# Gathered rows of x transposed by SyncE DMA instead of TensorE, with smaller key, value and query buffers, in a retention + top-1 expert kernel

## The chip, the cores and the metric

The kernel runs on one core of one Trainium2 chip. The metric is the device time of one execution in microseconds (us), lower is better. Three executions of the kernel before took 371.51, 374.61 and 376.12 us; the median is 374.61. Each profile shows one execution.

The engines are named as the profile names them: PE is TensorE (matmuls; PEld its weight loads), DVE is VectorE, ACT is ScalarE, POOL is GpSimd and SP is SyncE, which only issues DMAs here.

## What is computed

```python
# attention without softmax, 8 batches x 8 heads x 576 tokens x 64
scores = scale * np.matmul(q, k.transpose(0, 1, 3, 2))
Dmat = np.where(rel >= 0, gamma[:, None, None] ** rel[None, :, :], 0.0)   # decay by distance
attn_out = np.matmul(scores * Dmat[None], v)
x = attn_out.transpose(0, 2, 1, 3).reshape(4608, 512)

# one expert of eight for each token
logits = x @ w_gate
expert_idx = np.argmax(logits, axis=1)          # gate_w: that expert's softmax probability
for e in range(8):
    mask = expert_idx == e
    h = np.maximum(x[mask] @ w1[e], 0.0)        # 512 -> 1024
    out[mask] = gate_w[mask, None] * (h @ w2[e])  # 1024 -> 512
```

All inputs and the output are float32 in HBM. The kernel keeps x as bf16 rows in HBM (`x_rows`), and the experts work in bf16.

## The kernel before, in words

The kernel has two stages, written out in a fixed order: each engine runs its instructions in the order in which the program issues them, and no scheduler moves them.

**Attention stage (0 to about 202 us).** Forty blocks are walked: 8 batches, each four blocks of 128 tokens and one of 64. The loop at L693 runs block i, and in it prepares later blocks. POOL multiplies queries and keys by their decay (`scale_q` L244, `scale_k` L254), PE transposes the scaled tiles (`stage_TQ`, `stage_TK`), forms scores (`stage_SC`, output `pssc`, masked by DVE into `sc` at L311), the running state (`stage_S`, output `pss`) and the result (`stage_AV` and `stage_IN`, output `psx`), and turns that into rows (`stage_R`), which ACT copies into `xr` tiles (L397, L398) and SP writes to `x_rows` (L399, L405). SP also loads everything: keys for block i+6 early in iteration i (`load_k`, ordered after the latest mask step), values for block i+6 late (`load_v`, ordered after the latest copy of the result), and half a batch of queries at two places in each batch (`load_q`, two batches ahead). The pools are `ldq` (2 tiles of a whole batch), `ldk` (7 key tiles and 7 value tiles) and smaller working pools.

The logits are computed as the blocks come (`stage_L1`, `stage_L2`). When the first half of the batches is done, the routing of the first half of the tokens runs in small steps between the blocks (`route_first`, L655): the best expert for each token, the token's rank within its expert, and tables of row numbers (`tidg`) for each expert. Then, in four steps with a block between them, POOL gathers the rows of experts 0 to 3 (`gather`, an indirect DMA at L637 for each 128 rows into a tile `xg` of 128 x 512 bf16, pool `gath` of 8 tiles). From the last seven blocks on POOL also issues loads of the experts' weights, which convert to bf16 on the way.

**Expert stage (about 202 to 366 us).** It has sixteen units (`seq`, L745): each expert has a unit of 256 rows (ph 0, tokens of the first half) and one of 384 rows (ph 1, the rest). First come (0,0) to (3,0), then (0,1) to (3,1), then both units of experts 4 to 7. One unit is:

- `trans` (L756): for each 128 rows, PE transposes four 128 x 128 pieces of `xg` into PSUM (`pt`, pool `psT`, 2 buffers) and DVE copies them to `xt` (L764);
- `mm1` (L767): 32 matmuls `pm<-xt,w1b`, with ACT's ReLU into `ht` (L780), PSUM pool `psH` with 3 buffers;
- `mm2` (L784): 8 matmuls for each 128 rows, `py<-w2b,ht`; DVE multiplies by the gate into `ys` (L794), and POOL scatters the rows to the output (L795).

The order in PE's queue is `mm1` of a unit, `trans` of the next unit, `mm2` of the unit, except that the unit (0,1) is transposed after `mm2` of (3,0). The routing of the second half of the tokens (`route_rest`) runs on DVE and PE in small steps inside the first four units; its tables are needed to gather any ph 1 unit. After it, `gather` is called for (0,1) and (1,1), and from unit 4 on each unit i gathers the rows of unit i+2, behind `mm1`. Weights of experts 4 to 7 are fetched two loads per unit from the start of the stage (`fetch`). A check at the end (L858) covers experts with more rows than fit; its branch isn't taken with these inputs.

Of the kernel before, what the change touches and what calls it, by code (L numbers as in the profile page):

```python
# [41 lines left out]
def kernel(  # L42
# [33 lines left out]

    wpool = ctx.enter_context(tc.tile_pool(name="wts", bufs=4))
    rt = ctx.enter_context(tc.tile_pool(name="route", bufs=1))
    gp = ctx.enter_context(tc.tile_pool(name="gath", bufs=8))

    p1 = ExitStack()
    ldq = p1.enter_context(tc.tile_pool(name="ldq", bufs=2))
    ldk = p1.enter_context(tc.tile_pool(name="ldk", bufs=7))
    wkp = p1.enter_context(tc.tile_pool(name="wk", bufs=2))
    wk3 = p1.enter_context(tc.tile_pool(name="wk3", bufs=3))
    wk4 = p1.enter_context(tc.tile_pool(name="wk4", bufs=4))
# [10 lines left out]

    def load_q(b, g, dep=None, eng=None):

        if g == 0:  # L100
            qts[b] = ldq.tile([P, H, NCH, DH], F32, tag="q", name="qt")
        hs = slice(g * NP, (g + 1) * NP)
        after((eng or nc.sync).dma_start(out=qts[b][:, hs, :, :],
                                         in_=q[b, hs, 0:NCH * P, :].rearrange("h (p s) d -> p h s d", p=P)), dep)

    def load_kv(store, tag, src, i, dep):
        b, c = blocks[i]
        store[i] = ldk.tile([P, H, DH], F32, tag=tag, name=tag + "t")
# [16 lines left out]
    def load_v(i, dep=None):  # L125

        if i >= NB:
            return
        b, c = blocks[i]
        if c < NCH:  # L130
            load_kv(vts, "v", v, i, dep)
            return
        vts[i] = ldk.tile([P, H, DH], F32, tag="v", name="vt")
# [107 lines left out]
    def scale_q(b, p):  # L241
        h0 = 2 * p
        qq = wkp.tile([P, NCH, P], F32, tag="qq")
        nc.gpsimd.tensor_tensor(  # L244
            out=qq[:, :, :].rearrange("p s (h d) -> p h s d", d=DH), in0=qts[b][:, h0:h0 + 2, :, :],
            in1=qg[:, 0:NCH, h0:h0 + 2].rearrange("p s h -> p h s").unsqueeze(3)
                .to_broadcast([P, 2, NCH, DH]), op=ALU.mult)
        qqs[(b, p)] = qq
# [47 lines left out]
    def stage_SC(i):  # L296
# [1 line left out]
            return  # L298
        b, c = blocks[i]
        kT = kTs.pop(i)  # L300
        sc = wkp.tile([P, 2, NP, P], F32, tag="sc")
        scs[i] = sc
        if c < NCH:
            qT = qTs[b]
# [321 lines left out]
        slots[ph] = (tids, tidg, gat)  # L626


    gat_t = {}

    def gather(e, ph):
        nb = (CA if ph == 0 else CB) // P
        nr = NTOK // 2 if ph == 0 else NTOK
        for j in range(nb):
            i = j * E + e
            xg = gp.tile([P, DM], BF16, tag="xg", name="xg")
            nc.gpsimd.indirect_dma_start(  # L637
                out=xg[:, :], out_offset=None, in_=x_rows[0:nr, :],
                in_offset=bass.IndirectOffsetOnAxis(ap=slots[ph][1][:, i:i + 1], axis=0),
                bounds_check=nr - 1, oob_is_err=False)  # L640
            gat_t[(e, ph, j)] = xg

    def steps(g, budget):

# [8 lines left out]
        return True  # L653

    def route_first():  # L655
        incl = yield from softmax_top1(0, rtmp)
        yield from ranks(0, incl, rtmp, lambda: psw.tile([P, 512], F32, tag="W", name="psrk"))
        yield from prep(0, 0, rtmp)
        yield from rows_hot(0, 0, rtmp)
        yield from place(0, rtmp, lambda: psw.tile([P, 512], F32, tag="W", name="pspl"))  # L660
        for e in range(NA):
            yield None
            gather(e, 0)
        yield from prep(1, 0, rt)
        yield from rows_hot(1, 0, rt)

# [58 lines left out]
    while steps(rf, 1.0):  # L725
# [19 lines left out]
    seq = ([(e, 0) for e in range(NA)] + [(e, 1) for e in range(NA)]  # L745
           + [(e, ph) for e in range(NA, E) for ph in (0, 1)])
    xts = {}
    wq = [(e, i) for e in range(EW, E) for i in range(4)]

    def fetch(n):  # L750
        for _ in range(n):
            if wq:
                e, j = wq.pop(0)
                load_w(e, j, 2, wpool2)

    def trans(e, ph):  # L756
        nb = (CA if ph == 0 else CB) // P
        xt = xtp.tile([P, NPT, nb * P], BF16, tag=f"xt{ph}", name="xt")
        for j in range(nb):
# [4 lines left out]
            nc.vector.tensor_copy(out=xt[:, :, j * P:(j + 1) * P], in_=pt[:, :, :])  # L764
        xts[(e, ph)] = xt

    def mm1(e, ph, between):  # L767
        nb = (CA if ph == 0 else CB) // P
# [38 lines left out]
    trans(0, 0)  # L807
    rr = route_rest()
    steps(rr, 2.0)
    routed, late = [], []  # L810

    def route_on(n):
        more = steps(rr, n)
        if not more and not routed:
            routed.append(True)
            gather(0, 1)
            if late:
                gather(*late.pop())
        return more

    for i, (e, ph) in enumerate(seq):
        nxt = seq[i + 1] if i + 1 < len(seq) else None
        fetch(2)

        def during1():
            if i < NA:
                route_on(0.9)

        def during2():
            if i < NA:  # L830
                route_on(1.2)

        ht = mm1(e, ph, during1)
        if nxt == (0, 1):
            while route_on(1):
                pass
            mm2(e, ph, ht, during2)
            trans(*nxt)
        else:
            if nxt:  # L840
                trans(*nxt)
            if i >= NA and i + 2 < len(seq):
                gather(*seq[i + 2])
            elif nxt == (NA - 1, 0):
                late.append((1, 1))
                if routed:
                    gather(*late.pop())
            mm2(e, ph, ht, during2)
    p2.close()


# [103 lines left out]
```

## Time and profile before

| | |
|---|---|
| median of three executions | 374.61 us |
| profiled execution, its own time | 381.34 us |
| its span, first to last instruction | 379.6 us |
| start of the expert stage (first `pt`) | 202.3 us |
| start of the last `py` group | 361.0 us |
| PE, DVE, ACT, POOL busy | 331.8, 156.9, 127.1, 196.9 us |
| mean granted clock of PE | 0.963 |
| DMA share 202 to 245, 245 to 290, 290 to 366 us | 0.97, 0.81, 0.28 |

Busy time is the time in which an engine has at least one instruction running; idle time of an engine that doesn't set the end costs nothing. The slices divide the span into 40 equal parts of 9.5 us, and each digit is a busy share in tenths. The DMA share is the mean busy share of the core's 16 DMA engines. In a timeline row the columns are the start in us, the length in us, the engine, the line of the program, the operation and its tiles, and, in brackets, the idle time just before and who ended it. The largest groups of DMA issues, with the median time from issue to landing where the profile has it:

```profile
kt<-in_k_dram SPq DMA_DIRECT2D x32, 256.0 KB, 4.2
qt<-in_q_dram SPq DMA_DIRECT2D x14, 512.0 KB, 5.4
x_rows<-xr SPq DMA_DIRECT2D x32, 128.0 KB, 5.5
```

### The profile page before, as it was taken

Reading aid. Unit: us, or ns where it says so; the run is one execution under the profiler, and the core shown is the slowest. Engines: PE = TensorE matmul, PEld = TensorE weight load, DVE = VectorE, ACT = ScalarE, POOL = GpSimd, SP = SyncE. Lnnn points to the kernel's source line nnn. Section 1 sums busy time; section 2 is a strip of 40 time slices with the busy share of each in tenths; the row PEclk is TensorE's granted clock in tenths of the full one; section 3 lists DMA queues with packets and bytes.
Section 4 is the critical chain, followed back from the end, with each engine's and each line's share of the span. In section 5 each row is a group of like instructions: output and inputs, shape, how many; then the busy total and the mean of one; then the engine's idle time right before and its main releaser. Section 6 shows DMA issues by size and latency. Waiting matters only on the chain.

```text
span 379.6 us, 11084 instructions
## 1 busy us (share of the span) xinstructions
PE 331.8 (87%) x4642; PEld 241.9 (64%) x4642; DVE 156.9 (41%) x358; ACT 127.1 (33%) x292; POOL 196.9 (52%) x241
## 2 busy tenths in 40 slices
PE   2499999999999999987865998799999999999950
PEld 2378788878878787875754675355556565656520
DVE  3034443434346776732587872222223232323220
ACT  2234444343354344322321321134432323232300
POOL 4884452634345452568843357547666555554230
PEclk9799999999999999999996999899999999999995
DMA  8969888889799978699999898987679222223120
GB/s 211 254 108 224 213 207 202 202 213 199 193 209 224 231 186 205 161 190 232 213 207 213 181 191 212 186 168 143 175 190 207 97 98 96 101 95 108 55 74 7
DMA packets 113083, 65.34 MB, mean 172 GB/s; under 512 B 83838, under 2 KB 105342, under 8 KB 113024
## 3 DMA queue, kind: packets, MB, share of 16 engines
q0 software_dynamic: 18176, 31.47, 38.0%
q1 hardware_dynamic: 93792, 32.02, 36.3%
q10 hardware_dynamic: 1056, 1.05, 0.9%
q8 instruction: 38, 0.62, 0.7%
q14 instruction: 21, 0.17, 0.1%
HBM read 67.14 MB, written 15.20 MB: 217 GB/s over the span
## 4 chain that ended last, share of the span: by engine, by line
PE 78%; DMA 4%; ACT 4%; DVE 4%; POOL 3%; issue 2%; another core or an unknown queue 1%; SPq 0%; ACTq 0%; POOLq 0%; DVEq 0%
PE pm L60 19%; PE py L60 18%; PE psx L60 12%; PE pssc L60 7%; PE psr L63 5%; PE psk L63 5%; PE pss L60 5%; PE psq L63 2%; PE pt L63 2%; PE psl L60 2%; DMA x_rows<-xr 1%; DMA kt<-in_k_dram 1%; DMA vt<-in_v_dram 1%; DVE xt L764 1%; ACT kT L276 1%
## 5 line engine op out<-in xcount | busy, mean ns | idle before, releaser
L780 ACT ACTIVATE ht<-pm 128x384 bf16<-128x384 f32 (+1 forms) x96 | 50.5, 526 | 105.2 <-PE pm L60 95.5
L254 POOL TENSOR_TENSOR kk<-kt,kg 128x512 f32<-128x512 f32 x40 | 41.9, 1048 | 78.0 <-PE pss L60 47.7
L60 PE MATMUL pm<-xt,w1b 128*128 128x256 bf16 (+1 forms) x512 | 74.0, 304 | 2.2 <-DVE xt L764 2.2
L795 POOL DMA_INDIRECT out_dram<-ys,tids x40 | 40.9, 1022 | 67.5 <-DVE ys L794 61.4
L60 PE MATMUL py<-w2b,ht 128*128 128x512 bf16 x320 | 73.6, 385 | 2.5 <-issue 1.6
L60 PEld LDWEIGHTS <-w1b 128*128 128x128 bf16 x512 | 50.8, 99 | 25.0 <-DVE xt L764 2.0
L60 PEld LDWEIGHTS <-ht 128*128 128x128 bf16 x320 | 31.0, 99 | 38.3 <-issue 4.3
L794 DVE TENSOR_SCALAR ys<-py,gat 128x512 f32<-128x512 f32 x40 | 30.0, 750 | 50.3 <-PE py L60 46.7
L637 POOL DMA_INDIRECT xg<-x_rows,tidg x40 | 41.5, 1037 | 14.6 <-issue 9.8
L276 ACT COPY kT<-psk 128x512 f32<-128x512 f32 x40 | 23.8, 596 | 70.5 <-PE psk L63 41.8
L311 DVE TENSOR_TENSOR sc<-pssc,mask 128x1024 f32<-128x1024 f32 x32 | 39.1, 1222 | 19.6 <-issue 13.3
L356 DVE COPY xT<-psx 128x512 f32<-128x512 f32 x32 | 22.1, 692 | 54.8 <-PE psx L60 49.7
L60 PE MATMUL psx<-sc,vt 128*64 128x128 f32 (+1 forms) x640 | 37.6, 266 | 1.0 <-DVE sc L311 1.0
L63 PE MATMUL psk<-ident,kk 128*128 128x128 f32 x160 | 27.5, 294 | 11.9 <-POOL kk L254 11.3
L60 PE MATMUL pssc<-qT,kT 64*64 64x128 f32 (+1 forms) x1024 | 36.5, 255 | 1.2 <-issue 1.2
L764 DVE COPY xt<-pt 128x512 bf16<-128x512 bf16 x40 | 15.7, 420 | 51.4 <-PE pt L63 49.2
L244 POOL TENSOR_TENSOR qq<-qt,qg 128x512 f32<-128x512 f32 x32 | 33.9, 1061 | 1.3 <-DMA qt<-in_q_dram 0.8
L60 PEld LDWEIGHTS pssc<-qT,kT 64*64 64x64 f32 x1024 | 30.0, 135 | 3.8 <-issue 3.8
L60 PEld LDWEIGHTS psx<-sc,vt 128*64 128x64 f32 (+1 forms) x640 | 30.0, 136 | 3.2 <-DVE sc L311 2.2
L63 PEld LDWEIGHTS psk<-ident,kk 128*128 128x128 f32 x160 | 17.6, 145 | 17.3 <-POOL kk L254 12.6
L293 ACT COPY se<-pss 128x256 f32<-128x256 f32 x32 | 12.2, 380 | 36.8 <-PE psx L60 22.8
L60 PE MATMUL pss<-vt,kk 128*64 128x64 f32 x512 | 22.4, 231 | 0.0
(118 smaller groups left out, 340.1 us busy)
## 6 DMA issues: line engine op xcount, KB each, us to landing
kt<-in_k_dram SPq DMA_DIRECT2D x32, 256.0 KB, 4.2
vt<-in_v_dram SPq DMA_DIRECT2D x32, 256.0 KB
qt<-in_q_dram SPq DMA_DIRECT2D x14, 512.0 KB, 5.4
x_rows<-xr SPq DMA_DIRECT2D x32, 128.0 KB, 5.5
w1b<-in_moe_w_dram POOLq DMA_DIRECT2D x16, 256.0 KB
w2b<-in_moe_w_dram POOLq DMA_DIRECT2D x16, 256.0 KB
w1b<-in_moe_w_dram POOLq DMA_DIRECT2D x8, 512.0 KB
w2b<-in_moe_w_dram POOLq DMA_DIRECT2D x8, 512.0 KB
```

What stands on the lines that cost most here:

```text
L60: nc.tensor.matmul(out=out, lhsT=lhsT, rhs=rhs, start=start, stop=stop, skip_group_check=True)
L63: nc.tensor.transpose(out=out, in_=in_, identity=identity)
L244: nc.gpsimd.tensor_tensor(out=qq[:, :, :].rearrange("p s (h d) -> p h s d", d=DH), in0=qts[b][:, h0:h0 + 2, :, :], in1=qg[:, 0:NCH, h0:h0 ...
L254: nc.gpsimd.tensor_tensor(out=kk[:, :, :], in0=kts.pop(i)[:, :, :], in1=kg[:, blocks[i][1], :].unsqueeze(2).to_broadcast([P, H, DH]), op=A ...
L276: mark["kT"] = nc.scalar.copy(out=kT[:, :, :].rearrange("p a t -> p (a t)"), in_=pst[:, :])
L311: mark["sc"] = nc.vector.tensor_tensor(out=sc[:, :, :, :].rearrange("p j a i -> p j (a i)"), in0=pssc[:, :, :], in1=mask[:, :, :].rearrang ...
L356: mark["xT"] = nc.vector.tensor_copy(out=xTs[b][:, c, :].rearrange("p (w t) -> p w t", w=2), in_=psx[:, :, 0:2 * P])
L637: nc.gpsimd.indirect_dma_start(out=xg[:, :], out_offset=None, in_=x_rows[0:nr, :], in_offset=bass.IndirectOffsetOnAxis(ap=slots[ph][1][:, ...
L764: nc.vector.tensor_copy(out=xt[:, :, j * P:(j + 1) * P], in_=pt[:, :, :])
L780: nc.scalar.activation(out=ht[:, f0:f0 + per, :], in_=pm[:, :, :], func=AF.Relu)
L794: nc.vector.tensor_scalar(out=ys[:, :], in0=py[:, :], scalar1=gat[:, i:i + 1], scalar2=None, op0=ALU.mult)
L795: nc.gpsimd.indirect_dma_start(out=next(outs)[:, :], out_offset=bass.IndirectOffsetOnAxis(ap=tids[:, i:i + 1], axis=0), in_=ys[:, :], in_o ...
```

## The change

PE no longer transposes gathered rows. A new function `turn` has SP issue one DMA transpose for each gathered tile, from `xg` to `xt` in SBUF. `trans`, its PSUM tile `pt` and DVE's copy are gone. For the units (0,0) to (3,0) the transposes are issued in the attention stage, each expert's one step after its gather, into a pool `xta` of four tiles; for the other units `turn` directly follows `gather`, into a pool `xtb` of three tiles. A list `todo` orders the later gathers: as soon as the second routing is done, units 4 and 5; then at the start of unit i, before its `mm1`, unit i+2.

To make room, the pools shrink: `gath` from 8 to 6 tiles, keys from 7 to 4, values from 7 to 6, queries from 2 whole batches to 3 half batches, and `sc` and `ht` from 2 buffers to 1. In PSUM `psT` goes from 2 to 1 buffer and `psH` from 3 to 4. The first routing's temporaries move to another pool.

```diff
-    gp = ctx.enter_context(tc.tile_pool(name="gath", bufs=8))
+    gp = ctx.enter_context(tc.tile_pool(name="gath", bufs=6))
+    gpa = ctx.enter_context(tc.tile_pool(name="xta", bufs=NA))
...
-    ldq = p1.enter_context(tc.tile_pool(name="ldq", bufs=2))
-    ldk = p1.enter_context(tc.tile_pool(name="ldk", bufs=7))
+    ldq = p1.enter_context(tc.tile_pool(name="ldq", bufs=3))
+    ldk = p1.enter_context(tc.tile_pool(name="ldk", bufs=4))
+    ldv = p1.enter_context(tc.tile_pool(name="ldv", bufs=6))
...
-        if g == 0:
-            qts[b] = ldq.tile([P, H, NCH, DH], F32, tag="q", name="qt")
         hs = slice(g * NP, (g + 1) * NP)
-        after((eng or nc.sync).dma_start(out=qts[b][:, hs, :, :],
+        qts[(b, g)] = ldq.tile([P, NP, NCH, DH], F32, tag="q", name="qt")
+        after((eng or nc.sync).dma_start(out=qts[(b, g)][:, :, :, :],
...
-        sc = wkp.tile([P, 2, NP, P], F32, tag="sc")
+        sc = wk1.tile([P, 2, NP, P], F32, tag="sc")
...
+    def turn(e, ph):
+
+        nb = (CA if ph == 0 else CB) // P
+        xt = gps[ph].tile([P, NPT, nb * P], BF16, tag="xt", name="xt")
+        for j in range(nb):
+            nc.sync.dma_start_transpose(out=xt[:, :, j * P:(j + 1) * P], in_=gat_t.pop((e, ph, j))[:, :])
+        xts[(e, ph)] = xt
+
...
-        incl = yield from softmax_top1(0, rtmp)
-        yield from ranks(0, incl, rtmp, lambda: psw.tile([P, 512], F32, tag="W", name="psrk"))
+        incl = yield from softmax_top1(0, rt)
+        yield from ranks(0, incl, rt, lambda: psw.tile([P, 512], F32, tag="W", name="psrk"))
...
         for e in range(NA):
             yield None
             gather(e, 0)
+            if e > 0:
+                turn(e - 1, 0)
+        yield None
+        turn(NA - 1, 0)
...
-    xtp = p2.enter_context(tc.tile_pool(name="xtp", bufs=2))
-    htp = p2.enter_context(tc.tile_pool(name="htp", bufs=2))
+    gpb = p2.enter_context(tc.tile_pool(name="xtb", bufs=3))
+    htp = p2.enter_context(tc.tile_pool(name="htp", bufs=1))
...
-    psT = p2.enter_context(tc.tile_pool(name="psT", bufs=2, space=PSUM))
-    psH = p2.enter_context(tc.tile_pool(name="psH", bufs=3, space=PSUM))
+    psT = p2.enter_context(tc.tile_pool(name="psT", bufs=1, space=PSUM))
+    psH = p2.enter_context(tc.tile_pool(name="psH", bufs=4, space=PSUM))
...
-    def trans(e, ph):
-        nb = (CA if ph == 0 else CB) // P
-        xt = xtp.tile([P, NPT, nb * P], BF16, tag=f"xt{ph}", name="xt")
-        for j in range(nb):
-            xg = gat_t.pop((e, ph, j))
-            pt = psT.tile([P, NPT, P], BF16, tag="pt")
-            for c in range(NPT):
-                tr(pt[:, c, :], xg[:, c * P:(c + 1) * P], identb[:, :])
-            nc.vector.tensor_copy(out=xt[:, :, j * P:(j + 1) * P], in_=pt[:, :, :])
-        xts[(e, ph)] = xt
...
+    def gather_upto(i):
+        while todo and todo[0][0] <= i and (1 in slots or todo[0][1][1] == 0):
+            u = todo.pop(0)[1]
+            gather(*u)
+            turn(*u)
...
     for i, (e, ph) in enumerate(seq):
-        nxt = seq[i + 1] if i + 1 < len(seq) else None
         fetch(2)
+        if i >= NA:
+            gather_upto(i + 2)
...
         def during1():
             if i < NA:
                 route_on(0.9)
+                gather_upto(NA + 1)
...
         ht = mm1(e, ph, during1)
-        if nxt == (0, 1):
+        if i == NA - 1:
             while route_on(1):
                 pass
-            mm2(e, ph, ht, during2)
-            trans(*nxt)
...
+            gather_upto(NA + 1)
+        mm2(e, ph, ht, during2)
```

More of the change, by code (lines that the diff above doesn't have):

```diff
@@ L107, in load_kv @@
         b, c = blocks[i]
-        store[i] = ldk.tile([P, H, DH], F32, tag=tag, name=tag + "t")
+        store[i] = (ldk if tag == "k" else ldv).tile([P, H, DH], F32, tag=tag, name=tag + "t")
         after(nc.sync.dma_start(out=store[i][:, :, :],
@@ L132, in load_v @@
             return
-        vts[i] = ldk.tile([P, H, DH], F32, tag="v", name="vt")
+        vts[i] = ldv.tile([P, H, DH], F32, tag="v", name="vt")
         for u in range(2):
@@ L244, in scale_q @@
         nc.gpsimd.tensor_tensor(
-            out=qq[:, :, :].rearrange("p s (h d) -> p h s d", d=DH), in0=qts[b][:, h0:h0 + 2, :, :],
+            out=qq[:, :, :].rearrange("p s (h d) -> p h s d", d=DH), in0=qts[(b, p // 2)][:, h0 % NP:h0 % NP + 2, :, :],
             in1=qg[:, 0:NCH, h0:h0 + 2].rearrange("p s h -> p h s").unsqueeze(3)
@@ L626, in place @@
         slots[ph] = (tids, tidg, gat)
-    gat_t = {}
+    gat_t, xts = {}, {}
+    gps = [gpa]
     def gather(e, ph):
@@ L746 @@
            + [(e, ph) for e in range(NA, E) for ph in (0, 1)])
-    xts = {}
+    gps.append(gpb)
     wq = [(e, i) for e in range(EW, E) for i in range(4)]
@@ L805, in route_rest @@
         yield from place(1, rtm2, lambda: psT.tile([P, 512], F32, tag="pt", name="pspl"))
-    trans(0, 0)
     rr = route_rest()
     steps(rr, 2.0)
-    routed, late = [], []
-    def route_on(n):
[L813 to L819, printed above, removed]
+    todo = list(enumerate(seq))[NA:]
+    more = [True]
+    def gather_upto(i):
[3 more added lines that the diff above has]
+            turn(*u)
+    def route_on(n):
+        if more[0]:
+            more[0] = steps(rr, n)
+        return more[0]
     for i, (e, ph) in enumerate(seq):
-        nxt = seq[i + 1] if i + 1 < len(seq) else None
         fetch(2)
+        if i >= NA:
+            gather_upto(i + 2)
         def during1():
@@ L831, in during2 @@
                 route_on(1.2)
+                gather_upto(NA + 1)
         ht = mm1(e, ph, during1)
-        if nxt == (0, 1):
+        if i == NA - 1:
             while route_on(1):
                 pass
-            mm2(e, ph, ht, during2)
-            trans(*nxt)
[L839 to L848, printed above, removed]
+            gather_upto(NA + 1)
+        mm2(e, ph, ht, during2)
     p2.close()
```

## The prediction

> **What bounds the kernel now.** I read the busy table and the slices first. TensorE (PE) is busy 87% of the span and at 9 in nearly every slice; no other engine passes 52%. The chain of waits, by engine and by line, is the same engine: PE holds 78%, and the line to watch is `pt`, the transposes of the gathered rows, with the DVE copy `xt` that empties them.
>
> ```profile
> PE 331.8 (87%) x4642; PEld 241.9 (64%) x4642; DVE 156.9 (41%) x358; ACT 127.1 (33%) x292; POOL 196.9 (52%) x241
> PE   2499999999999999987865998799999999999950
> ...
> DMA  8969888889799978699999898987679222223120
> ```
>
> The attention stage ends at 202 us, the expert stage runs from there to 366. In the expert stage the timeline of PE alone says what a transpose costs, better than its busy time, since busy spans of a pipelined engine overlap. Two seams between a first product (`pm`) and a second (`py`):
>
> ```profile
> 202.30 1.06 PE L63 MATMUL pt<-identb,xg 128*128 128x128 bf16 x8
> 205.06 5.33 PE L60 MATMUL pm<-xt,w1b 128*128 128x256 bf16 x32 [1.70 <-DVE xt L764]
> ...
> 250.53 0.61 PE L63 MATMUL pt<-identb,xg 128*128 128x128 bf16 x8
> 251.43 0.38 PE L63 MATMUL pt<-identb,xg 128*128 128x128 bf16 x4 [0.29 <-DVE xt L764]
> 251.65 5.34 PE L60 MATMUL py<-w2b,ht 128*128 128x512 bf16 x24
> ...
> 285.04 0.61 PE L63 MATMUL pt<-identb,xg 128*128 128x128 bf16 x8
> 285.48 5.34 PE L60 MATMUL py<-w2b,ht 128*128 128x512 bf16 x24
> ```
>
> Columns are start, length, instruction. From the start of `pt` to the start of what follows is the price of a seam: 0.44 us with two blocks (285.04 to 285.48), 1.12 with three (250.53 to 251.65), the third block waiting for one of two PSUM buffers.
>
> **What the Trainium skill says.** "VectorE: DVE Perf Modes", The three transpose paths, prices a 128x128 bf16 transpose at 390 ns on TensorE and 1309 ns by the DMA crossbar. The trace has 219 ns for TensorE (median of 160 `pt`), and in a stream 8 cost 0.44 us; no DMA transpose is in it. "Advanced Engine Details and Errata", X-Bar Transpose (TRN2), calls transposing DMAs as fast as ordinary ones; "DMA: Bandwidth & Descriptors", Latency and other measured facts, has 261 GB/s measured on one kernel. The same page's Anatomy of one DMA gives about 2 us fixed to a GpSimd DMA; here an SP write of the same 128 KB (`x_rows<-xr`) lands after 5.5 us. These differ by a lot for one block of 128x512 bf16: 0.50 us of all 16 engines at 261 GB/s, or 4 x 1309 ns = 5.2 us if blocks follow one another. The forecast hangs on that.
>
> **The change part by part.**
>
> *Removed:* 160 PE transposes and 40 copies. The sixteen seams, read as above in order: 2.76 (202.30 to 205.06, which includes DVE waiting for the last `x_rows` write to land, because `xt` lies where `xr` lay), 0.96, 0.44, 0.45, 2.23 (243.10 to 245.33, here after the second product), 1.12, 1.13, 1.12, 0.44, 1.23, 0.45, 1.26, 0.44, 1.23, 0.45, 1.12. Sum **16.8 us**, all on PE and so on the path. DVE loses 40 x 0.42 = 16.8 us of copies; it is at 12.8 of 45 us from 245 to 290, so that is worth nothing by itself.
>
> *Added:* 40 DMA transposes on SP's queue, eight in the last blocks of attention, 32 later. SP has no loads left then: before, its queue is empty from 199 to the end. What the eight are queued among is the last `x_rows` writes. Transpose pair e waits for gather e; the gathers are issued at 166.4, 171.8, 177.6 and 184.2 us, a pair of issues each. With six gather buffers the fourth gather also waits for the first transposes, about 175 to 180, before its old place. The last writes may slip by some us behind the fourth gather; ACT's `xr` copies have four buffers (some 20 us), and the write's readers come at 227. The first transposed rows are due at 202, over 20 us after their gather. One new reader of that queue: a DVE step of the second routing (`blk`, 211.8 us) waits for all of it, since its tile lies on memory of the stage before. The last write lands at 204.1 now; it would have to slip 5 us to count. I take 0, range 0 to 4.
>
> *The fifth unit* (expert 0, second half) has the tightest date. Its rows can be gathered only after the second routing: now at 227.16 us. The first four seams are gone by then (4.6 us), so about 222.6. A gather behind two weight loads has been used at most 8.5 us after its issue with no wait (issue 286.72, third block used 295.17). Last issue about 225.2, landed by 233.7 at the latest, plus one transpose of 2.5 us (my estimate from that page, 2.0 + 0.5) to 5.5 (the `x_rows` landing): 236.2 to 239.2. Due: 245.33 less five seams (6.84) = 238.5. I take 0.5, range 0 to 6.
>
> *Later units:* the gather is issued two units ahead, 17 to 21 us, instead of one. From gather landing (about 10 us after the unit's start with two weight loads ahead of it) some 7 to 10 us are left for three transposes.
>
> *DMA:* 40 x 0.50 = 20 us of all engines. The share is 0.81 from 245 to 290 and 0.28 from 290 to 366: free are 8.6 + 54.7 us; 15 transposes in the first stretch need 7.5, the rest 8.5. It fits, narrowly at first; weights slowed there are due tens of us later (loads of expert 4 start at 203.7, its first use is at 290.7). Before 202 the share is over 1, and eight add 4 us of transfer to writes and loads with slack. I take 0.5 us for contention, range 0 to 4.
>
> *Smaller buffers,* all taken at zero, each with its cover: keys 7 to 4 buffers make load i+6 wait for the scaling of block i+2, done one iteration earlier (POOL 25.4 to 26.4 for the load issued at 30.9); values 6: the load already waits for the block it replaces; half query tiles: the first to wait is issued at 12.4 us, its buffer is free at 8.9; one `sc` buffer and one `ht` buffer: PE itself is in order, the reader precedes the writer's products. If a cover failed, a key load would be late and PE idle by up to its 4.2 us landing, several times: up to +10. Without transposes `py` starts directly after `pm`; its last contraction block is wanted 7 x 0.213 = 1.5 us in, the last ACT needs 0.5 to 0.6. Four `pm` buffers instead of three: gain at most the 2.5 us of PE waits near 238, whose ACT wait has no releaser that the profile knows; I count none.
>
> *Sum:* -16.8 + 0.5 + 0.5 + about 0.8 for small new waits at sixteen unit starts = **-15 us**. The profiled execution took 381.34 us (span 379.6, 1.7 around it), the median of three is 374.61, and the seams are PE work that both have: 374.6 - 15 = **360 us**.
>
> **The rivals.**
>
> *Partly hidden (363 to 371):* transposes of 2 to 4 us each under the weight loads. 15 blocks in four units of 10.4 us allow 2.8 us each at first; at 4 us they miss by up to 15 x 1.2 = 18 us, less the lead of about 8: ten of the 15 are lost, and 370 remains. For: the DMA share of 0.81. Against: 261 GB/s.
>
> *The transposes become the bound (slower, about 416):* 32 follow one another from about 231 us. At 5.2 us each the last ends at 397, then its unit (10.4) and the tail after the last `py` (379.6 - 366.3 = 13.3): span 421, 41 us more, 416 on the median. The point where nothing is gained: 379.6 - 13.3 - 10.4 = 355.9, less 231, by 32: 3.9 us each; a loss of over 2% from 4.1. For: the 1309 ns and the absence of any such row in this trace. Against: the two statements of the skill; and nothing here shows that such a DMA would use fewer engines than a copy of 128 partitions.
>
> *SP's queue blocks attention:* a transpose waiting 10 us more for its gather holds back writes, and through ACT's `xr` and the routing steps up to 8 us: 368.
>
> *It does not do what it says:* if each transpose waited for all other DMAs it would be the serial case; the waits in the built program are the gather, the buffer's reader and the DMA eight places back, so I give it nothing apart.
>
> **How the numbers follow.** Hidden 0.62 (355 to 363); partly hidden 0.12 and blocked queue 0.05 (363 to 371, half of each within 2%); crossbar-bound 0.20 (0.02 within 2%, and 0.18 slower, from 382 up to 416); buffers failing 0.01, slower. Two per cent, 7.5 us, is about what a measurement of this kernel tells from no change. Faster 0.70, within 0.11, slower 0.19. The range 355 to 386 leaves out the far end of the crossbar case (some 0.15) and a better gain than 16.8 + 2.5.
>
> **What would show it.** Right: no `pt` rows, `py` following `pm` within 0.2 us, PE waits on `xt` near zero from unit six on, unit 0's first product right after `psl` near 202, SP's transposes landing in under 3 us. Wrong: PE idle before `pm` released by the DMA `xt<-xg`, of near equal length in every unit (crossbar bound) or only near 238 (late fifth unit); PE gaps before 200 (buffers).

## The result, and the profile after

The changed kernel takes **395.91 us** (median of four executions, 392.83 to 398.13) beside 373.31 us (371.51 to 376.12) of the kernel before on the same chip: ratio 1.0592, 95% interval 1.0485 to 1.0699. It is 22 us slower; 15 us less was forecast. The profiled execution took 394.96 us, its span is 393.2 us, and the mean granted clock of PE is 0.942. The busy table and the slices of the changed kernel:

```profile
PE 330.5 (84%) x4482; PEld 235.6 (60%) x4482; DVE 141.3 (36%) x318; ACT 127.0 (32%) x292; POOL 197.0 (50%) x241
...
PE   2599999999989999997759289459997999999960
...
DMA  8969888889989987799999999997999955556310
```

PE has 160 instructions fewer, and DVE its 40 copies fewer, as the change says. But PE's slices (9.8 us each) now have holes at 216 us (2), from 246 to 265 us (4, 5) and at 295 us (7), and the DMA slices hold 9 almost without a break up to 315 us, where they had fallen to 2 from 294 on. The chain of waits of the changed kernel, in order of time (start, length, what held the end; lines between are left out), names what filled the holes:

```profile
209.94 14.10 DMA x_rows<-xr
...
237.74 8.81 DMA xg<-x_rows,tidg
249.38 10.51 DMA xt<-xg
...
287.14 10.32 DMA xt<-xg
```

In the kernel before every piece of that chain over 1 us is PE's from 205 us to the end, but for one of 2.25 us. Here it goes through four DMAs: a write of x rows that lands at 224.0, the gather of unit 4 (the fifth unit), and the transposes of units 4 and 7. PE's timeline of the changed kernel (start, length, in brackets idle time before and who ended it) gives the size of each hole:

```profile
225.35 3.40 PE L60 MATMUL py<-w2b,ht 128*128 128x512 bf16 x8 [7.29 <-DVE ys L797]
...
260.03 8.28 PE L60 MATMUL pm<-xt,w1b 128*128 128x384 bf16 x32 [10.31 <-DMA xt<-xg]
268.14 5.34 PE L60 MATMUL py<-w2b,ht 128*128 128x512 bf16 x24
...
297.59 8.27 PE L60 MATMUL pm<-xt,w1b 128*128 128x384 bf16 x32 [3.34 <-DMA xt<-xg]
```

The seams are gone: `py` at 268.14 follows `pm` at 260.03 as soon as that has run. The holes are three. In unit 1 (the second unit), PE waits 7.29 us for a `py` buffer, which DVE empties late, since DVE itself stands at the routing step `blk` (the row of its waits below). The routing matmuls `pspl` that follow take 5.4 us instead of 2.1. Before unit 4 PE waits 10.31 us for `xt`, before unit 7 3.34. And the first product after each of these two holes runs 8.28 and 8.27 us instead of 5.36, while the granted clock is low (0.85 on average from 245 to 290 us). Lost: 7.3 + 3.3 + 1.7 (a slow `pm` at 234.87) + 10.3 + 2.9 + 3.3 + 2.9 = 31.7 us. Less the 16.8 us of seams, that is 14.9 of the 22.6 us between the medians.

This pair of profiles hides most of the rest, because the profiled execution of the kernel before was itself a long one (381.34 us). Its last `psl`, with which attention ends, starts at 201.85 us, and it has some 4 us of PE stalls near 238. In the profiles of runs 5, 7 and 8 below, which have no DMA transposes in attention, that `psl` starts at 196.4 to 197.3 us; in the changed kernel it starts at 202.82. The row of run 5, then of the changed kernel:

```profile
196.42 0.66 PE L63 MATMUL psl<-ident,lt 128*128 128x128 f32 x2 [3.18 <-DVE lt L419]
202.82 0.66 PE L63 MATMUL psl<-ident,lt 128*128 128x128 f32 x2 [4.35 <-DVE lt L420]
```

So some 6 us more are probably lost before the expert stage begins, about 21 us in all. The largest new gap of PE there, 2.4 us at 183 us, names no releaser that the profile knows.

SP's queue of the changed kernel shows where the last two of the early eight transposes stand (length is the time in which the group was issued):

```profile
199.94 4.12 SPq L650 DMA_TRANSPOSE xt<-xg  x2
204.15 4.82 SPq L400 DMA_DIRECT2D x_rows<-xr  x2
...
246.71 11.00 SPq L650 DMA_TRANSPOSE xt<-xg  x6
```

The last writes of x rows were issued at 198 to 199 us before; they now stand behind the fourth pair and go out at 204 to 211, and the first two pairs land only 13.2 and 13.5 us after their issue. Of DVE's waits the changed kernel has a new one, and its DMA issues have a new row (count, median us from issue to landing):

```profile
DVE blk L565 <- DMA x_rows<-xr: 13.5, 1, 13.5
...
xt<-xg SPq DMA_TRANSPOSE x40, 5.9
```

Last, the DMA engines. By stretch of time the columns are length, busy us of five engines, clock, DMA share and GB/s; first the kernel before, then the changed one:

```profile
180.00:190.00 10.00, 8.89 (x177) 7.53 (x181) 5.15 (x12) 3.12 (x8) 8.42 (x12) 1.00 1.09 212
190.00:245.00 55.00, 44.07 (x451) 30.42 (x441) 34.73 (x113) 12.36 (x25) 27.10 (x32) 0.91 1.01 195
245.00:290.00 45.00, 43.79 (x265) 24.21 (x265) 12.83 (x23) 15.71 (x32) 28.35 (x30) 1.00 0.81 176
```

```profile
180.00:190.00 10.00, 7.61 (x172) 6.33 (x170) 3.23 (x6) 2.92 (x8) 5.73 (x7) 1.00 1.42 121
190.00:245.00 55.00, 39.52 (x343) 26.50 (x342) 29.95 (x105) 10.64 (x22) 25.60 (x33) 0.84 1.18 206
245.00:290.00 45.00, 34.69 (x178) 17.96 (x177) 6.01 (x8) 13.14 (x27) 24.30 (x27) 0.85 0.94 182
```

From 166 to 180 us the share is 1.14 before and 1.18 after, at 227 and 216 GB/s. Multiplied out (share by length, 166 to 290 us), the share makes 118.9 us for these 124 before and 137.9 now, 19 us more. Some twenty transposes fall into the stretch (the early eight and those of units 4 to 7), so about 1 us of all 16 engines each, if the share is taken as engine time. It can't be quite that, since it stands over 1; the bytes (rate by length) are 23.9 MB before and 23.8 now. The share rose for no more bytes, the transposes' own among them. Between 180 and 190, where the first two pairs are under way, the share rises to 1.42 while the rate falls from 212 to 121 GB/s.

### The profile page after: what moved, and what is told of

Its sections match the earlier page's. It is cut to its first block, busy times and chain, and to the rows that moved or that the text cites. A ratio compares the mean times of both kernels' runs of the same rounds, so it can differ in the third digit from the quotient of the medians.

```text
span 393.2 us, 10815 instructions
## 1 busy us (share of the span) xinstructions
PE 330.5 (84%) x4482; PEld 235.6 (60%) x4482; DVE 141.3 (36%) x318; ACT 127.0 (32%) x292; POOL 197.0 (50%) x241
## 4 chain that ended last, share of the span: by engine, by line
PE 65%; DMA 14%; DVE 7%; POOL 4%; ACT 4%; issue 3%; SPq 1%; POOLq 0%; ACTq 0%; DVEq 0%
PE pm L60 16%; PE py L60 13%; PE psx L60 12%; PE pssc L60 6%; DMA xt<-xg 5%; PE pss L60 5%; PE psk L63 5%; PE psr L63 5%; DMA x_rows<-xr 4%; DMA xg<-x_rows,tidg 2%; PE psl L60 2%; PE psq L63 2%; DVE rh L594 2%; DVE pay L584 1%; DMA kt<-in_q_dram 1%
## 5 line engine op out<-in xcount | busy, mean ns | idle before, releaser
L60 PE MATMUL pm<-xt,w1b 128*128 128x256 bf16 (+1 forms) x512 | 82.1, 324 | 13.7 <-DMA xt<-xg 13.7
L60 PEld LDWEIGHTS <-w1b 128*128 128x128 bf16 x512 | 53.9, 106 | 42.1 <-issue 21.1
L277 ACT COPY kT<-psk 128x512 f32<-128x512 f32 x40 | 23.8, 596 | 70.6 <-PE psk L63 44.9
L60 PE MATMUL pssc<-qT,kT 64*64 64x128 f32 (+1 forms) x1024 | 35.2, 255 | 2.4 <-issue 2.4
L60 PEld LDWEIGHTS pssc<-qT,kT 64*64 64x64 f32 x1024 | 29.2, 135 | 4.3 <-issue 4.3
L63 PEld LDWEIGHTS psk<-ident,kk 128*128 128x128 f32 x160 | 17.4, 144 | 16.8 <-POOL kk L255 12.5
L294 ACT COPY se<-pss 128x256 f32<-128x256 f32 x32 | 12.2, 381 | 35.1 <-PE psx L60 21.8
L233 POOL DMA_DIRECT2D w2b<-in_moe_w_dram x24 | 18.2, 764 | 9.5 <-DMA w2b<-in_moe_w_dram 7.8
```

Of the source, the lines that this page charges most:

```text
L60: nc.tensor.matmul(out=out, lhsT=lhsT, rhs=rhs, start=start, stop=stop, skip_group_check=True)
L63: nc.tensor.transpose(out=out, in_=in_, identity=identity)
L233: after(nc.gpsimd.dma_start(out=wb[e][part // n][:, o:o + m, :], in_=w[e, o * P:(o + m) * P, :].rearrange("(c p) f -> p c f", p=P)), dep)
L277: mark["kT"] = nc.scalar.copy(out=kT[:, :, :].rearrange("p a t -> p (a t)"), in_=pst[:, :])
```

## The experiments

The theory after this profile: a DMA transpose is dear beside weight loads, and the DMA engines were busy without a break until about 290 us; what the transposes take there comes back as late weights, late x rows, late gathers and late transposes. Rivals: the new wait of `blk` alone does the harm; the smaller buffers do; a transpose is slow whatever runs beside it. All times are medians; the ratio is to the kernel before on the same chip in the same hours (373.25 us for the first four runs, 372.53 for the next four, 384.44 for the last four, whose chip is slower; only ratios compare across).

| run | us | ratio, 95% interval |
|---|---|---|
| routing memory moved | 392.56 | 1.0483 (1.0422 to 1.0545) |
| weights fetched later | 397.92 | 1.0659 (1.0575 to 1.0742) |
| plain copies for transposes | 375.03 | 1.0062 (1.0024 to 1.0100) |
| small buffers alone | 382.29 | 1.0251 (1.0207 to 1.0295) |
| the same, gather pool of 8 | 370.67 | 0.9956 (0.9933 to 0.9980) |
| DMA transposes, units 8 to 15 only | 366.80 | **0.9850 (0.9806 to 0.9894)** |
| DMA transposes, units 4 to 15 only | 377.69 | 1.0112 (1.0063 to 1.0161) |
| DMA transposes, units 0 to 3 only | 390.88 | 1.0140 (1.0068 to 1.0212) |
| both moves at once | 392.31 | none: 382.74 to 395.92 |
| changed kernel without weights 1 to 7 | 371.56 | 0.9689 (0.9633 to 0.9744) |
| kernel before without weights 1 to 7 | 383.00 | 0.9955 (0.9933 to 0.9976) |

**1. The wait of `blk` taken away.** The second routing's scratch pool is opened after the other pools of the stage, so that it no longer lies on the `xr` tiles that the late writes read.

```diff
-    rtm2 = p2.enter_context(tc.tile_pool(name="rtm2", bufs=1))
...
+    rtm2 = p2.enter_context(tc.tile_pool(name="rtm2", bufs=1))
```

> The changed kernel with one line moved: the pool of the second routing's tiles is created after the output pool, so that its first tile no longer lies where the rows of x wait for their write to HBM. Theory (the 13.5 us that DVE waits at the routing step blk for the last x_rows write, which SP issues behind the early transposes, stop PE): the wait at blk is gone, the 7.3 us gap of PE inside the second py group of unit 1 is gone, the placing matmuls take 2 to 3 us instead of 5.4, 10 to 12 us gained: 384 to 386 us. The 10.3 us wait before unit 4 stays, 8 to 11 us, since its gather and transposes meet the same weight loads. Rival (the memory of x is only where DVE happens to wait, and PE is late because the DMA engines are full): less than 3 us gained.

The wait of `blk` and the hole in unit 1 are gone, `pspl` is back at 2.26 us, and yet the time falls only from 395.91 to 392.56 us (1.059 to 1.048 of the kernel before, with intervals that overlap). PE's timeline of this run has the answer. The profiled execution is the longest of the four, and its attention ends 7.7 us later (last `psl` at 210.54 instead of 202.82), so times are compared from there:

```profile
228.61 2.26 PE L60 MATMUL pspl<-pay,rh 128*128 128x120 bf16 x40
...
265.79 7.96 PE L60 MATMUL pm<-xt,w1b 128*128 128x384 bf16 x32 [21.89 <-issue]
```

Counted so, PE comes to unit 4 some 13 us sooner and waits there 21.9 us instead of 10.3. The gather goes out 30.5 us after that `psl` (at 241.03) instead of 34.9 (at 237.74); POOL's queue still stands at weight loads until 225 us. Unit 4 starts 55.2 us after it instead of 57.2. So of the waits removed, 2 us come out, not the theory's 10 to 12. A wait ahead of a longer one was removed.

**2. The weights put off.** `fetch(2)` runs only from the fifth unit on.

```diff
-        fetch(2)
         if i >= NA:
+            fetch(2)
             gather_upto(i + 2)
```

> The changed kernel, but the weights of experts 4 to 7 are fetched during units 4 to 11 instead of 0 to 7. Theory (the gather of unit 4 stands behind two weight loads on POOL's queue and its transposes share the engines with two more, so 8.8 us and 10.5 us instead of 4 to 5 and 3 to 5): the wait of PE before unit 4 falls from 10.3 us to under 3; the transposes of unit 7 and later may become late instead by some us; the gap at blk in unit 1 is hardly changed (6 to 9 us). Net 7 to 11 us gained: 385 to 389 us. Rival (each crossbar transpose has its own cost of 4 us or more, whatever else moves): wait before unit 4 over 8 us, under 3 us gained.

Unit 4 starts without a wait (`pm` at 245.09). The waits came back later: 17.9 us of PE on `xt` in three places, the first of them before unit 6

```profile
271.25 7.52 PE L60 MATMUL pm<-xt,w1b 128*128 128x384 bf16 x32 [5.24 <-DMA xt<-xg]
```

and the time is 397.92 us, no gain (even the shortest two of the four executions, 393.86 and 395.75, are no better than the changed kernel's 392.83 to 398.13). It looks like a sum of DMA work that doesn't fit, and not like a single misplaced wait.

**3. The same DMAs as plain copies.** Each transpose is replaced by an ordinary copy of the same 128 KB in the same place; the rows stay untransposed, so the products are others.

```diff
-            nc.sync.dma_start_transpose(out=xt[:, :, j * P:(j + 1) * P], in_=gat_t.pop((e, ph, j))[:, :])
+            nc.sync.dma_start(out=xt[:, :, j * P:(j + 1) * P],
+                              in_=gat_t.pop((e, ph, j))[:, :].rearrange("p (c t) -> p c t", t=P))
```

> The changed kernel with a plain DMA copy of xg to xt in place of each DMA transpose: same queue, same order, same waits, same bytes; the rows are not transposed, so the experts multiply the wrong layout. Theory (queue order and full DMA engines decide, and the crossbar takes about twice a copy's engine time): landing falls from a median of 5.9 us to 3 to 5, the blk gap of 7.3 us stays above 4, the wait before unit 4 stays above 4 us; 3 to 9 us gained: 387 to 393 us. Rival (the crossbar itself is slow): both waits nearly vanish and the time goes to 365 to 372 us.

375.03 us, 21 us less than with transposes. Bytes, queues, order and buffers are the same, so 21 us are due to the kind of DMA. Neither the theory's 387 to 393 us nor the rival's 365 to 372 came true. The stretch from 180 to 190 us and the landing in this run:

```profile
180.00:190.00 10.00, 8.67 (x196) 7.09 (x192) 5.62 (x12) 2.53 (x7) 6.58 (x9) 1.00 1.19 228
...
xt<-xg SPq DMA_DIRECT2D x40, 128.0 KB, 3.2
```

228 GB/s instead of 121, and 3.2 us to land instead of 5.9; from 166 to 290 us 26.7 MB are moved, where the changed kernel moved 23.8. Attention ends as early as without such DMAs, within 2 us (last `psl` at 198.20). Still it is no faster than the kernel before, though the seams of 16.8 us are gone: `blk` waits 6.0 us for the last write, the routing matmuls take 6.9 us instead of 2.1, and waits of 2.0 us before unit 4 and 5.4 before unit 5 remain, each with a slow product behind it. So of the 39 us that the change loses (22.6 and the 16.8 won back), the kind of DMA accounts for 21. About 18 stay with copies in their place; how much of that is the added bytes and how much the order of the queues was not tried.

**4 and 5. The small buffers alone,** in the kernel before, first with all of them, then with the gather pool left at 8 tiles (the first two lines of the diff undone; queries, `sc` and `ht` shrink as in the change in both).

```diff
-    gp = ctx.enter_context(tc.tile_pool(name="gath", bufs=8))
+    gp = ctx.enter_context(tc.tile_pool(name="gath", bufs=6))
-    ldk = p1.enter_context(tc.tile_pool(name="ldk", bufs=7))
+    ldk = p1.enter_context(tc.tile_pool(name="ldk", bufs=4))
+    ldv = p1.enter_context(tc.tile_pool(name="ldv", bufs=6))
```

> The kernel before with the changed kernel's smaller buffers alone (gather 6, keys 4, values 6, query half tiles 3, one sc and one ht buffer), transposes on TensorE as before. Theory (the covers of the prediction hold): within 1% of the kernel before, 370 to 377 us. Rival (a key or value load becomes late): PE waits on kt, vt or qt in the attention stage, 3 us or more slower.

> As the run of the smaller buffers alone, but with the gather pool at 8 tiles again: key, value, query, sc and ht buffers small. Theory (the 9 us of that run came from POOL, which waited 14.5 us for a gather buffer that PE freed only in the expert stage): within 1% of the kernel before, 370 to 377 us. Rival (keys, values or queries): still 378 us or more.

The first run was 2.5% slower, against the expectation. POOL's row in it shows why, and that it is no fault of the changed kernel:

```profile
197.49 1.07 POOL L637 DMA_INDIRECT xg<-x_rows,tidg  x1 [14.48 <-PE pt L63]
```

With transposes on PE the gather tiles of unit 0 are read only when the expert stage begins (197 us in this run), so the seventh gather waits for a tile, and POOL's weight loads behind it. With eight gather tiles, and everything else small, the time is 370.67 us: these buffers cost nothing. The pool of six in the changed kernel wasn't tried apart.

**6. The DMAs by themselves.** After the last unit of the kernel before, stages were added: loads of `w1` that convert to bf16 (512 KB written), 24 DMA transposes of a 128 x 512 bf16 tile, and 24 copies of it, alone and together. `loads` issues on POOL, `turns` (DMA transposes into eight tiles in turn) and `copies` on SP; in `ready` DVE reads each target. Only these stages are read.

```diff
+    loads(16)
+    ready(wd)
+    turns(24)
+    ready(td)
+    copies(24)
+    ready(wd + td)
+    loads(16)
+    turns(24)
+    ready(wd + td)
+    loads(16)
+    copies(24)
+    ready(wd + td)
```

> The kernel before with five stages added behind its expert stage, each waiting for the one before: 16 loads of 512 KB of weights by POOL alone; 24 DMA transposes of one 128x512 tile by SP alone; 24 plain copies of the same tile by SP alone; 16 loads with 24 transposes; 16 loads with 24 copies. Only the added stages are read, not the total. Theory (a transpose takes the shared DMA engines for about 1 us and slows every other queue meanwhile): loads alone 35 to 45 us, transposes alone about 30 (SP's issue of 1.2 us each), copies alone about 15; loads with transposes at least 20 us longer than loads alone; loads with copies 5 to 12 us longer. Rival (a transpose costs the engines no more than its bytes, 0.3 to 0.5 us): loads with transposes at most 10 us longer than alone.

SP's queue and the DMA share of the stages (the stages overlapped otherwise than planned: the second group of loads ran beside the first copies, and the last copies ran when the loads were done):

```profile
443.39 31.40 SPq L870 DMA_TRANSPOSE td<-bsrc  x24
476.62 32.22 SPq L874 DMA_DIRECT2D td<-bsrc  x24
523.28 130.73 SPq L870 DMA_TRANSPOSE td<-bsrc  x24
669.03 15.27 SPq L874 DMA_DIRECT2D td<-bsrc  x24
```

```profile
412.00:443.00 31.00, 0.00 (x0) 0.00 (x0) 1.46 (x14) 0.00 (x0) 0.00 (x0) 0.50 1.09 205
444.00:476.00 32.00, 0.00 (x0) 0.00 (x0) 1.51 (x14) 0.00 (x0) 0.00 (x0) 0.50 0.49 98
...
525.00:654.00 129.00, 0.00 (x0) 0.00 (x0) 2.80 (x26) 0.00 (x0) 13.34 (x18) 0.50 1.13 205
670.00:684.00 14.00, 0.00 (x0) 0.00 (x0) 1.30 (x14) 0.00 (x0) 0.00 (x0) 0.50 0.59 204
```

Alone, a transpose takes 1.3 us (31.40 / 24) and 0.65 us of all engines (0.49 x 32 / 24); a copy takes 0.64 us (15.27 / 24) and, by its share of 0.59, 0.38 us of all engines. SP itself needs 1.2 us to issue a transpose and 0.6 a copy, so alone both go as fast as SP issues them. Loads alone have a share of 1.09, one landing every 4.96 us. Beside loads a copy takes 1.34 us (32.22 / 24), but **a transpose 5.4 us** (130.73 / 24), four times as long as alone: about one transpose for each load. That is above the 2.8 us allowed in units 4 to 7 and above the 3.9 us at which the prediction's slower rival loses everything.

What a transpose takes from the loads is much less. They are spaced 5.7 us instead of 4.96, so in these 130.73 us they lose 17 us to 24 transposes, 0.7 us each: between the theory's 20 and the rival's 10, and less than the 1 us that the theory gave a transpose. The rate is 205 GB/s with transposes as without. The fall of the rate in the kernel (121 GB/s) doesn't show here.

**7 to 9. Only some units by DMA.** In the kernel before (its buffers kept), `turn` is issued behind the gather for units 8 to 15 (shown), then, without the condition, for 4 to 15; in a third kernel (that of run 5, with the first routing's temporaries where the change puts them) only for units 0 to 3, in the attention stage.

```diff
             if i >= NA and i + 2 < len(seq):
                 gather(*seq[i + 2])
+                if i + 2 >= 8:
+                    turn(*seq[i + 2])
```

> The kernel before with its own buffers; only units 8 to 15 (experts 4 to 7) are turned by DMA, each right after its gather, two units ahead; units 0 to 7 on TensorE as before. Theory (transposes hurt where the DMA engines are full; from unit 8 on the share was 0.28): PE never waits for xt in units 8 to 15, the eight seams of 6.6 us go, 365 to 369 us. Rival (a transpose is late or disturbs whatever the load): PE waits on xt, 372 us or more.

> The kernel before with its own buffers; units 4 to 15 are turned by DMA, units 0 to 3 on TensorE, so no transpose is issued in the attention stage. Theory (twelve transposes for units 4 to 7 meet the weight loads of experts 4 to 7): PE waits before units 4 to 7 for 5 to 12 us in all, nothing is gained over the run with units 8 to 15 alone: 367 to 377 us. Rival (only the eight early ones in the attention stage do harm): 358 to 363 us.

> The kernel before with the small key, value and query buffers; only the eight blocks of units 0 to 3 are transposed by DMA, in the attention stage, the other 32 on TensorE as before. Theory (transposes beside full weight queues take from the other queues): the seams of units 0 to 3 go (2.76 + 0.96 + 0.44 + 0.45, some 4.6 us, part of it), but the DMA rate between 180 and 190 us falls from 212 GB/s towards 121, the weight loads of experts 0 to 3 leave POOL's queue 5 to 15 us later and the gather of unit 4 is issued later than 227 us: 373 to 382 us, no gain. Rival (the early eight are harmless, all the loss lies in units 4 to 7): 366 to 370 us, the gather of unit 4 issued by 228 us and no wait of PE on it.

Units 8 to 15 by DMA: 366.80 us, faster than both kernels. Their eight seams are 6.6 us of the prediction's sum; 5.6 us are won (1.5% of 372.53). The transposes landed in 2.4 to 4.1 us, and PE waited for them once:

```profile
287.55 5.36 PE L60 MATMUL pm<-xt,w1b 128*128 128x384 bf16 x32 [0.48 <-DMA xt<-xg]
```

The first five of them (269.4 to 286 us) came while the last weights were loading, at a share of 0.95 and 1.00 (265 to 275 and 275 to 285 us), and landed in 2.7 and 4.1 us where the profile has it. So a high share alone doesn't make a few of them late.

Units 4 to 7 added: the seams of this kernel are worth 12.2 us, and it is 4 us slower than the kernel before. Its first row of PE on `xt`:

```profile
245.70 7.52 PE L60 MATMUL pm<-xt,w1b 128*128 128x384 bf16 x32 [10.65 <-DMA xt<-xg]
```

With 2.2 us of slow product, and waits of 2.88 and 1.87 us later, 17.6 us are lost, against the 16.4 (12.2 + 4.2) to be explained. The early eight were not part of this kernel: the wait before unit 4 is there without them.

Units 0 to 3 alone: ratio 1.0140, beside 0.9956 for the kernel that it is built on: 1.8% or 7 us slower, though seams of 4.6 us are dropped. Attention ends 7 us later than in the runs without weights on the same chip (last `psl` at 209.1 instead of 201.8 us); PE's gaps there name no releaser that the profile knows, so that part isn't explained. From there on the gather of unit 4 takes 29.5 us to go out (at 238.58) instead of 25.3 before. DVE stands at `blk` for 8.9 us, and the rate in 190 to 200 us is 132 GB/s at a share of 1.35, here with eight gather tiles.

**10. Both moves of runs 1 and 2 at once.**

> The changed kernel with both moves at once: the routing's scratch memory away from the tiles that the late writes read, and the third weight fetch put off to the fifth unit. Theory (the sum of DMA work before 290 us is what does not fit): the waits move once more, 386 to 394 us, at best some 5 us under the changed kernel, DMA share over 0.95 from 166 to 270 us. Rival (two separate waits, each of which the other edit had uncovered): both are gone, 370 to 378 us.

Inconclusive in size: the four executions spread from 382.74 to 395.92 us beside 384.44, so 0.996 to 1.030, where the theory's times stand for ratios of 1.034 to 1.056 and the rival's for 0.99 to 1.013. The profile, of the longest of the four, has the waits in new places, as the theory says: none before unit 4, but 15.5 us of PE on `xt` in four later places, the longest, 6.96 us, at 344.56. The shortest execution, at 0.996, would fit the rival. So part of the loss may be a matter of order; how much stays open.

**11 and 12. The weight loads left out.** In the changed kernel and in the kernel before all experts use the weights of expert 0, so the loads of experts 1 to 7 don't take place.

```diff
     def load_w(e, part, n, pool, dep=None):
+        if e > 0:
+            wb[e] = wb[0]
+            return
```

> The changed kernel with the weight loads of experts 1 to 7 left out (all experts use the weights of expert 0, so this part of the computation is changed). Theory (a transpose is slow only beside weight loads): the 40 transposes land in 2.4 to 4 us, no wait of PE on xt of over 1 us, and the time is 12 to 18 us below that of the kernel before with the same loads left out. Rival (a transpose is slow whatever runs beside it, or its wait chain through the gather is too long): waits of several us before units 4 to 7 remain, and the time is no lower than that of the kernel before with the same loads left out.

> The kernel before with the weight loads of experts 1 to 7 left out in the same way, as the base of the run without weights of the changed kernel. Theory and rival alike: 365 to 374 us, since before the change no product waits for weights; the seams of 16.8 us stay.

371.56 beside 383.00 us: now the change **wins 11.4 us**, 3.0% (spans 368.2 and 382.1 us), and attention ends at the same time in both (last `psl` at 201.80 and 201.85). Where unit 4 ends and unit 5 begins in the changed kernel of this pair:

```profile
245.90 5.34 PE L60 MATMUL py<-w2b,ht 128*128 128x512 bf16 x23
251.08 5.36 PE L60 MATMUL pm<-xt,w1b 128*128 128x384 bf16 x32
```

No gap, no wait on `xt` anywhere, with the same 40 transposes, the early eight among them, the same queue and the same gathers. The DMA share from 245 to 290 us is 0.48, beside 0.26 in the run without weights of the kernel before. The rival of a transpose that is slow whatever runs beside it falls. The run doesn't tell what a transpose meets in the DMA engines from what its gather meets on POOL's queue, since both lose the loads. The gain expected was 12 to 18 us; the first seam is 1.2 us shorter without weights (1.58 instead of 2.76), and the other few us aren't resolved.

## Why the prediction was wrong

*The seams, -16.8 us:* right. They are gone in every unit, and where nothing else is late most of them come out as time: 5.6 of 6.6 us for the last eight, 11.4 of some 15.6 for all when the weights are left out.

*DMA, "it fits, narrowly":* **this step failed.** Its term was 0.50 us of all engines for a transpose and 2.5 us to land. Measured: 0.65 us alone and 0.7 us beside loads (what these lose in run 6; by the share in the changed kernel about 1 us), so 0.50 was too little by 30% or more. The time to land was missed by far more: 5.9 us median, 13 us for the first two pairs, one in 5.4 us when loads run beside. The free 8.6 us between 245 and 290 us were counted as room, and the early eight, laid where the share was over 1, were taken as covered by slack in writes and loads. From 166 to 290 us only 124 - 118.9 = 5 us were free by the share, and by the prediction's own 0.50 twenty transposes needed 10. For the last eight units, most of them past the weight loads, the estimate was good enough: 5.6 of their 6.6 us come out. The Trainium skill's X-Bar Transpose (TRN2) in "Advanced Engine Details and Errata", which the prediction leaned on, has a transposing DMA as fast as an ordinary one; here it took twice as long alone (1.3 and 0.64 us, as SP issued them) and four times as long beside loads (5.4 and 1.34 us).

*The early eight, 0 (0 to 4):* mis-sized. The write that had to slip 5 us to count slipped 20 (landing at 224.0 instead of 204.1), DVE stood at `blk` for 13.5 us and PE lost 7.3 and then 3.3 us. The chain was named rightly; the slip was priced by the order of SP's queue alone. POOL's weight loads were given slack, and not followed to the gather that stands behind them: they left its queue by 217 instead of 202 us. Run 1 shows that this second effect is the larger: without the wait of `blk` unit 4 starts only 2 us sooner. The 6 us lost in attention itself were at nothing too; "SP's queue blocks attention", with its 0.05 and up to 8 us, came near them in size. Its path, the `xr` copies held back, is there once (ACT waits 4.55 us for a write of x rows at 196 us), but isn't shown to be what held PE.

*The fifth unit, 0.5 (0 to 6):* mis-sized, by the two terms above. Last gather of the unit to be issued by 225.2, landed by 233.7, one transpose of 2.5 to 5.5 us after it: so it was put. Measured: first issue at 237.74, last `xt` landed at 259.9. PE waited 10.3 us, and paid 2.9 more by a slow clock, a term that the prediction lacked.

*Later units:* right from unit 8 on; unit 7 was late by 3.3 us.

*Contention, 0.5 (0 to 4):* the same failed estimate a second time. Without the weight loads the loss is gone; 21 us of it go with the kind of DMA (run 3).

*Small buffers, 0:* right for keys, values, queries, `sc` and `ht`, measured at 0.9956. The gather pool of six costs 2.5% where PE transposes. In the changed kernel POOL waits 3.9 us once for a tile (260.64), for a gather of unit 6, which PE then starts without a wait; and run 9, with eight tiles, has its weight loads leave POOL's queue by 217 us too, and the same kind of fall of the rate.

*The rivals:* the crossbar rival had nearly the right price, 5.2 us each, measured 5.4, but by luck: it was four blocks at 1309 ns, one after another, a property of the transpose. Alone the tile takes 1.3 us. The price is one of the company it keeps; so the serial time of 416 us did not come about, because after 290 us the price drops. "Partly hidden" had one right place (units 4 to 7), with 10 us lost there where run 8 loses 17.6. The forecast weighed the two as if the price were one number for the whole kernel.

## What to carry to other kernels

Before moving work from a compute engine to DMA, sum the DMA share over the stretch from where the transfers can start to where they are due. Where it is near or over 1 for long, as here from 166 to 245 us, what is added can come back as lateness in queues that the change doesn't touch. It is a warning and no rule: five transposes at a share near 1 did no visible harm here. Moving only the last eight units, most of them where the share was 0.29, was worth 1.5%, where moving all lost 5.9%. And measure the new DMA beside the traffic that it will meet, not alone: both what it takes from that traffic (0.7 us here) and how long it waits itself (5.4 us).

## What the runs showed that was not expected

- A DMA transpose of a 128 x 512 bf16 tile within SBUF lands every 1.3 us alone and every 5.4 us beside converting weight loads, a copy of the same tile every 0.64 and 1.34 us. The loads lose 0.7 us to each transpose. What inside the DMA engines makes the difference was not tried, nor whether loads that don't convert do the same; that about one transpose passes per load is what the times say.
- While the early transposes were under way, the rate of all DMA fell to 121 GB/s at a share of 1.42 (before: 212 at 1.09; copies in their place: 228 at 1.19). In the added stages the rate didn't fall (205 GB/s, at 1.13), so what brings it down in the kernel stays open.
- After PE had waited 3.1 to 21.9 us for `xt`, its next 32 products of 384 columns took 6.7 to 8.3 us instead of 5.36 in these runs: a wait can cost up to 2.9 us more than its length. The Trainium skill, "TensorE: Matmul & The Clock Gate", What's actually happening, says that PE falls to half its clock after an idle window of about 3.4 us. Most of the waits agree; but 1.98 us before unit 4 in run 3 were enough (7.04 us, at a clock of 0.57 from 240 to 244), and 2.88 us in run 8 were not (5.36).
